# Attention and routed experts on one core: a group's output product in two passes of 256 tokens, weights' halves side by side

## The chip, the cores and the metric

The kernel runs on one core of a Trainium2 chip. The metric is the device time of one execution in microseconds (us). Three runs of the kernel before took 1854.25, 1854.31 and 1855.54 us; the median is 1854.31 us. A fourth, profiled execution took 1854.06 us, and all rows below are from it. The engines are named as the profile names them: PE is TensorE (matmuls; PEld are its weight loads), DVE is VectorE, ACT is ScalarE, POOL is GpSimd, SP is the engine that issues most DMAs.

## The reference

There are two stages. The first is attention of 4 x 12288 queries on 768 pooled keys; the second sends each token to one of 8 experts.

```
kv_flat = mean over 4x4 patches of kv @ w_sr            # k = v = kv_flat, 768 x 128 for each of 4 batches
s = (q @ k.T) / sqrt(128);  a = softmax(s);  x = a @ v  # 4 x 12288 tokens of 128
e_idx = argmax(x @ w_gate);  gate_w = softmax(x @ w_gate)[e_idx];  eom = sigmoid(x @ w_output_gate)
h  = relu(x[e] @ w1[e])                                  # 128 -> 1024
ye = h @ w2[e]                                           # 1024 -> 128
out[e] = gate_w * eom[e] * ye                            # for the tokens whose e_idx is e
```

## The kernel before

Tokens come in 96 groups of 512 (`GT`), 24 groups to a batch (`GPB`). The kernel guesses one expert for each batch, the one that most of its tokens choose, and runs all tokens of the batch through it; the few tokens with another expert are listed by indirect DMAs and done in small tiles at the end. Every fp32 product is made of fp16 parts: a number is held as a high half and a low half, and a product is high by high, high by low and low by high.

Three products of a group fill PE: the scores S (per block of 128 tokens 6 matmuls of 384 columns), the attention's output U (18 matmuls of 512 columns), and the expert. The expert has two: H, per block f of 128 of the 1024 hidden features 3 matmuls of 512 columns (`moe_h`, L938 to L940), and Y, the output product (`moe_y`, L948 to L977). For H, ACT writes the high half HH (`Relu`, L943), and DVE the low half HL (L945); both are 128x512 in fp16, in rings of 5 tiles each. For Y, HH and HL are the stationary operands: per f and per block j of 128 tokens, HH is multiplied with the high half of w2 and, in a second matmul with the same HH loaded again, with its low half; then HL with the high half of w2. These 12 matmuls of 128 columns all add into the same 128 columns of j. Four j of 128 fp32 fill one PSUM bank, tile Y of the pool psY, which has that one buffer. After the eighth f, ACT copies Y to `ys` in SBUF (L977), and Y is free for the next group. PSUM has eight banks: four for S (two tiles of two banks, psA), three for H and U (psH) and one for Y.

```
for j in range(GB):                       # L964 to L968
    for h in range(2):
        add(Y[:, ts(j, P)], HH[:, ts(j, P)], w2[:, h, :], ...)
for j in range(GB):
    add(Y[:, ts(j, P)], HL[:, ts(j, P)], w2[:, 0, :])
```

After the last attention group there is another form, called wide: the banks of S are free then, so Y takes two of them, and one matmul of 256 columns multiplies HH with both halves of w2, which lie side by side; the two results stand in different columns, and ACT (L974) and DVE (L975) add them.

Order is written out by hand. The main loop runs over groups i, with 8 slots s each; a slot issues, in the order of `cfg.ORD` = "shxryfue", the scores of a block of 128 (in even slots), one block of H, the exponential (even) or the rounding (odd), one block of Y, half of U (slots 5 and 6) and waiting events. Every engine runs its own instructions in the order in which they are issued. `hb` and `yb` count the blocks of H and Y. Y follows H by 4 blocks (5 for the first of a group); the last three blocks of a group come at the start of a slot, ahead of the scores. A group's H starts two groups after its attention (`LAG`), and one slot in 30 (one in 8 from group 72 on) has no H. When the attention is over, the last groups' H and Y are still open and follow by themselves. `moe_scale` (L985) multiplies `ys` with the gates 8 groups after the attention of its group, in the second half of a group's slots; `moe_out` stores it. `w_load` (L835) fetches an expert's weights.

Of the kernel before, what the change touches and what calls it, by code (L numbers as in the profile page):

```python
# [20 lines left out]
F32 = mybir.dt.float32  # L21
F32R = mybir.dt.float32r
F16 = mybir.dt.float16
# [98 lines left out]
def body(ctx, tc, q, kv, w_sr, w_gate, w_og, w1, w2, out, cfg=Cfg):  # L122
# [104 lines left out]


    kvst = {}
    KVN = [[0, 0] for _ in range(NB)]  # L230
# [312 lines left out]
    def qk(i, j):  # L543
# [288 lines left out]

    MSC, WT, WW2, HS, YP, OST, OT = {}, {}, {}, {}, {}, {}, {}
# [100 lines left out]
    def moe_h(i, f):  # L934
        w1h, w1l = WT[i // GPB][0:2]
        UH, UL = US[i]
        H = psH.tile([P, GT], F32, tag="H", name=f"H{i}_{f}")
        pe.matmul(H, w1h[:, ts(f, P)], UH, start=True, stop=False)  # L938
        pe.matmul(H, w1h[:, ts(f, P)], UL, start=False, stop=False)  # L939
        pe.matmul(H, w1l[:, ts(f, P)], UH, start=False, stop=True)  # L940
        HH = wk.tile([P, GT], F16, tag="HH", bufs=5, name=f"HH{i}_{f}")
        HL = wk.tile([P, GT], F16, tag="HL", bufs=5, name=f"HL{i}_{f}")
        ins = act.activation(HH, H, AF.Relu)  # L943
        pace[:] = [getattr(ins, "ins", ins).name]
        dve.scalar_tensor_tensor(HL, H, 0.0, HH, op0=ALU.max, op1=ALU.subtract)  # L945
        HS[(i, f)] = (HH, HL)

    def moe_y(i, f):  # L948
        HH, HL = HS.pop((i, f))
        if f == 0:  # L950
# [9 lines left out]
        for j in range(GB):  # L960
            if wide:
                add(Y[:, j // 2, ts(j % 2, 2 * C)], HH[:, ts(j, P)], w2, f == 0 and j % 2 == 0)
                continue
            for h in range(2):  # L964
                add(Y[:, ts(j, P)], HH[:, ts(j, P)], w2[:, h, :], f == 0 and j == 0 and h == 0)
        for j in range(GB):
            add(Y[:, j // 2, j % 2 * 2 * C:j % 2 * 2 * C + C] if wide else Y[:, ts(j, P)],
                HL[:, ts(j, P)], w2[:, 0, :])  # L968
        if f == NFB - 1:
            ys = wk.tile([P, GB, C], F32, tag="ys", bufs=OL + 2, name=f"ys{i}")  # L970
# [8 lines left out]
            del US[i]  # L979

# [159 lines left out]
    with tc.manual_schedule(engines={pool.engine, sp.engine, pe.engine, act.engine, dve.engine}):  # L1140
# [22 lines left out]
        tix, tgen = [], []  # L1163
        om = NG - OL - 1
        begun = False
# [115 lines left out]

        kl, kp, hb, yb = first()
        tpre = None

# [22 lines left out]
        for i in range(3, NG + OL + 1):  # L1307
# [5 lines left out]
            for s in range(8):  # L1313
# [6 lines left out]
                go = mi >= 0 and not (att and ((8 * i + s) % cfg.SK == cfg.SO if i < 72 else (8 * i + s) % 8 == 3))  # L1320
                for _ in range(1 + (cfg.YF and yb % 8 == 6)):
                    if go and yb % 8 >= 5 and yb < 8 * NG:
                        moe_y(*divmod(yb, 8))
                        yb += 1
                for o in cfg.ORD:
                    if o == "h" and go:
                        if hb < 8 * NG:
                            moe_h(*divmod(hb, 8))
                            hb += 1
                    if o == "s" and att and s % 2 == 0:  # L1330
                        qk(i, s // 2)
# [15 lines left out]
                    if o == "y" and go and yb == hb - 4 - (cfg.YE and hb < 8 * NG and yb % 8 == 0):  # L1347
                        for _ in range(1 + (yb == hb - 5)):
# [45 lines left out]
                routes(0, att and mi >= 0 and s % 2 == 1)  # L1394
                if not att and s % 2 and om < NG and om in OST and unit[om][0] in MSC:
                    moe_scale_all(om)
                    om += 1
                if NU - 1 in SCT and not tix:
# [49 lines left out]
```

## Time and profile before

| | us |
|---|---|
| median of three runs | 1854.31 |
| the profiled execution | 1854.06 |
| its span, first to last instruction | 1852.4 |
| PE busy in the span | 1820.7 (98%), 16465 matmuls |
| PEld busy | 1187.6 (64%) |
| DVE busy | 1451.5 (78%) |
| ACT busy | 1316.6 (71%) |
| POOL busy | 1323.3 (71%) |
| TensorE's granted clock over the span | 0.999 of full speed |

The gap between the span and the execution's time is 1.66 us. A PE row's own duration is modelled and overlaps that of the next; what a matmul takes is read from the distance between starts.

### The profile page before, as it was taken

To read this page: it belongs to the slowest core of one execution; us is meant where nothing else is said; L and a number is where in the kernel's file an instruction comes from. 1 tells how busy PE (TensorE), PEld (TensorE's weight loads), DVE (VectorE), ACT (ScalarE), POOL (GpSimd) and SP (SyncE) were. 2 spreads that over 40 slices of the span, in tenths; PEclk is the share of its full clock that TensorE was granted. 3 is DMA by queue.
4 is the path that set the end of the run, shared out by engine and by line. 5 is a ranking of instruction groups with operands and counts; after the bars stand their busy time and mean duration, and the time that the engine had idled before them with its cause. 6 is when DMAs were issued, how large, how long until landed. Compare 5 with 4: busy or idle time off the path is not lost. (4 is left out here: it accounts for less than half of the span.)

```text
span 1852.4 us, 43920 instructions
## 1 busy us (share of the span) xinstructions
PE 1820.7 (98%) x16465; PEld 1187.6 (64%) x16465; DVE 1451.5 (78%) x2856; ACT 1316.6 (71%) x2367; POOL 1323.3 (71%) x1563
## 2 busy tenths in 40 slices
PE   6999999999999999999999999999999999999998
PEld 5566666666666666666666666666666666666666
DVE  6876887788878777788787787878887777787774
ACT  4777777777776777777777776767687777777644
POOL 4546877866888878768588787786687786786841
PEclk9999999999999999999999999999999999999999
DMA  8999989989998988989988999888989899887822
GB/s 253 165 171 167 183 157 191 168 159 190 185 181 175 180 178 161 187 157 181 174 177 178 183 183 178 182 155 168 178 170 168 173 172 170 158 168 155 135 64 74
DMA packets 884070, 312.47 MB, mean 169 GB/s; under 512 B 827584, under 2 KB 833857, under 8 KB 883856
## 3 DMA queue, kind: packets, MB, share of 16 engines
q1 hardware_dynamic: 870944, 309.18, 85.4%
q0 software_dynamic: 12480, 0.40, 0.6%
q8 instruction: 130, 2.13, 0.5%
q14 instruction: 84, 0.69, 0.1%
q10 hardware_dynamic: 432, 0.07, 0.0%
HBM read 56.83 MB, written 51.25 MB: 58 GB/s over the span
## 5 line engine op out<-in xcount | busy, mean ns | idle before, releaser
L140 POOL TENSOR_TENSOR ph<-pr,ph 128x384 f16<-128x384 f32 x764 | 707.0, 926 | 335.4 <-issue 265.8
L945 DVE SCALAR_TENSOR_TENSOR HL<-H,HH 128x512 f16<-128x512 f32 x768 | 526.2, 686 | 162.4 <-ACT HH L943 151.9
L943 ACT ACTIVATE HH<-H 128x512 f16<-128x512 f32 x768 | 456.6, 595 | 265.5 <-PE H L940 255.7
L579 ACT ACTIVATE pr<-S,nm,qm 128x768 f32<-128x768 f32 x384 | 380.8, 992 | 188.0 <-DVE nm L568 170.9
L958 PEld LDWEIGHTS <-HH 128*128 128x128 f16 x5952 | 393.1, 98 | 139.8 <-issue 0.5
L820 POOL DMA_INDIRECT scr<-rw,idx x384 | 387.9, 1010 | 119.7 <-issue 62.7
L958 PE MATMUL Y<-w,HH 128*128 128x128 f16 (+1 forms) x5952 | 467.8, 221 | 0.2 <-ACT ys L977 0.2
L567 DVE TENSOR_REDUCE nm<-S 128x1 f32<-128x768 f32 x384 | 363.7, 947 | 71.5 <-PE S L565 69.8
L626 PE MATMUL U<-PT,V 128*128 128x512 f16 (+1 forms) x1746 | 404.3, 377 | 8.6 <-DMA PT<-ph 3.9
L596 ACT ACTIVATE ph<-pr 128x768 f16<-128x768 f32 x380 | 320.1, 842 | 1.2
L565 PE MATMUL S<-K,qT 128*128 128x384 f16 x1536 | 312.3, 326 | 0.0
L958 PE MATMUL Y<-w,HL 128*128 128x128 f16 x3072 | 296.9, 219 | 0.0
L938 PE MATMUL H<-U,w 128*128 128x512 f16 x768 | 291.0, 379 | 1.7 <-DVE HL L945 1.6
L939 PE MATMUL H<-U,w 128*128 128x512 f16 x768 | 291.0, 379 | 0.5 <-DVE U L631 0.5
L940 PE MATMUL H<-U,w 128*128 128x512 f16 x768 | 291.1, 379 | 0.2 <-POOL w L140 0.2
L626 PEld LDWEIGHTS <-V 128*128 128x128 f16 x1746 | 166.1, 98 | 189.8 <-issue 10.6
L565 PEld LDWEIGHTS <-qT 128*128 128x128 f16 x1536 | 150.1, 98 | 99.8 <-issue 0.4
L958 PEld LDWEIGHTS <-HL 128*128 128x128 f16 x3072 | 205.8, 98 | 1.2
L562 PE MATMUL S<-K,qT 128*128 128x384 f16 x768 | 187.6, 326 | 4.7 <-ACT pr L579 4.5
L631 DVE SCALAR_TENSOR_TENSOR U<-U,U 128x512 f16<-128x512 f32 x96 | 66.4, 692 | 91.4 <-ACT U L630 91.3
L940 PEld LDWEIGHTS <-w 128*128 128x128 f16 x768 | 75.1, 98 | 91.9 <-issue 0.8
L140 POOL TENSOR_TENSOR kvs<-kvs 128x256 f32<-128x256 f32 (+2 forms) x150 | 112.8, 752 | 24.1 <-DMA kvs<-in_kv_dram 13.1
(207 smaller groups left out, 1451.5 us busy)
## 6 DMA issues: line engine op xcount, KB each, us to landing
kvs<-in_kv_dram SPq DMA_DIRECT2D x96, 256.0 KB
q<-in_q_dram SPq DMA_DIRECT2D x96, 256.0 KB
urows<-uT SPq DMA_DIRECT2D x96, 256.0 KB
out_dram<-ys SPq DMA_DIRECT2D x96, 256.0 KB
PT<-ph SPq DMA_TRANSPOSE x384
scr<-rw,idx POOLq DMA_INDIRECT x384
wr<-in_moe_w_dram SPq DMA_DIRECT2D x8, 512.0 KB
tw<-in_moe_w_dram SPq DMA_DIRECT2D x4, 512.0 KB
```

The costliest lines, as they stand in the source:

```text
L140: ins = pool.tensor_tensor(*a, **k)
L565: pe.matmul(S[:, h, 0:384], x, k[:, ts(h, 384)], start=False, stop=(n == 1))
L567: dve.tensor_reduce(out=nm[:, 0:1], in_=S[:, :, 0:384], op=ALU.max, axis=AX.XY, negate=True)
L579: act.activation(pr.rearrange("p (a k) -> p a k", a=2), S[:, :, 0:384], AF.Exp, bias=nm[:, 1:2], scale=es, accum_out=SUMS[c][:, bl:bl + 1])
L596: act.activation(ph[:, 0, :], PR[(i, j)], AF.Copy)
L626: pe.matmul(PVP[i][:, cols], ops[n][0], ops[n][1][:, cols], start=(n == 0), stop=(n == len(ops) - 1))
L820: ins = pool.indirect_dma_start(out=scr, out_offset=bass.IndirectOffsetOnAxis(ap=idx[:, bl:bl + 1], axis=0), in_=rw[:, bl, :], in_offset=None,
L938: pe.matmul(H, w1h[:, ts(f, P)], UH, start=True, stop=False)
L940: pe.matmul(H, w1l[:, ts(f, P)], UH, start=False, stop=True)
L943: ins = act.activation(HH, H, AF.Relu)
L945: dve.scalar_tensor_tensor(HL, H, 0.0, HH, op0=ALU.max, op1=ALU.subtract)
L958: pe.matmul(o, h, w, start=first, stop=(f == NFB - 1), skip_group_check=True)
```

## The change

While the attention runs, a group's Y is made in two passes of 256 tokens (`moe_y2`). In a pass the one bank holds two blocks j, with 256 columns each: the first 128 for w2's high half and the next 128 for its low half, as in the wide form. HH is loaded once and multiplied with both halves in one matmul of 256 columns; HL with w2's high half adds into the first 128. After the eighth f of a pass, ACT copies the low part of the bank to `ys`, and DVE adds the high part to it; then the bank is free for the second pass. Group 0 and the groups that begin after the attention keep the old forms; in the built program 87 groups have the new one. Since a pass needs one half of the tokens of all eight f, HH and HL are no longer 5 tiles of 512 each: they are half tiles in one buffer HB, rings of 10 for the first 256 tokens and of 16 for the others. The order of Y follows a table `TY` of half blocks: two f go together as one step u, four steps make a pass, and after each pass come two slots with no Y. Beside that, `moe_scale` goes by a counter `sc` that waits for `ys` to be there, and an expert's weights are fetched into a buffer of `stg` (that of the kv staging) and not into one of their own.

```
@@ qk: which group is scaled
-        m = i - OL - 1
-        scale = (lambda: moe_scale(m, 2 * j - 4, 2 * j - 2)) if j >= 2 and m >= 0 else None
+        m = sc[0]
+        scale = None
+        if j >= 2 and (m in OST and m <= i - OL - 1 and j == 2 or j == 3 and sc[1]):
+            scale = lambda: moe_scale(m, 2 * j - 4, 2 * j - 2)
+            sc[1] = j == 2
+            sc[0] += j == 3
@@ rings
+    N1, N2, YSB = 10, 16, OL + 2
+    HB = cst.tile([P, 2, N1 + N2, GT // 2], F16, name="HB")
@@ w_load
-        t = kvp.tile([P, 2, FF], F32, tag="wr", bufs=1, name=f"wr{b}")
+        t = kvp.tile([P, 2, FF], F32, tag="stg", name=f"wr{b}")
@@ moe_h
-        HH = wk.tile([P, GT], F16, tag="HH", bufs=5, name=f"HH{i}_{f}")
-        HL = wk.tile([P, GT], F16, tag="HL", bufs=5, name=f"HL{i}_{f}")
+        a, b = (8 * i + f) % N1, N1 + (8 * i + f) % N2
+        HH, HL = (HB[:, h, a:b + 1:b - a, :] for h in range(2))
+        H = H.rearrange("p (h x) -> p h x", h=2)
...
+    def halved(i):
+        return HV.setdefault(i, 0 < i and now[0] < 8 * NG)
+
+    def moe_y2(i, u):
+        h, n = divmod(u, 4)
+        if u % 4 == 0:
+            YP[i] = (psY.tile([P, GT], F32, tag="Y", name=f"Y{i}_{h}") if now[0] < 8 * NG else
+                     psA.tile([P, 2, 512], F32, tag="A", name=f"Y{i}_{h}")[:, 0, :]).rearrange("p (j h c) -> p j h c", j=2, h=2)
+        Y = YP[i]
+        for f in (2 * n, 2 * n + 1):
+            HH, HL = (x[:, h, :] for x in HS[(i, f)])
+            w2 = WW2[i // GPB][:, :, ts(f, P)]
+            for j in range(2):
+                pe.matmul(Y[:, j, :, :], HH[:, ts(j, P)], w2, start=(f == 0 and j == 0), stop=(f == NFB - 1), skip_group_check=True)
+            for j in range(2):
+                pe.matmul(Y[:, j, 0, :], HL[:, ts(j, P)], w2[:, 0, :], start=False, stop=(f == NFB - 1), skip_group_check=True)
+        if n == 3:
+            if h == 0:
+                OS2[i] = wk.tile([P, GB, C], F32, tag="ys", bufs=YSB, name=f"ys{i}")
+            ys = OS2[i][:, 2 * h:2 * h + 2, :]
+            act.activation(ys, Y[:, :, 1, :], AF.Copy)
+            dve.tensor_tensor(ys, Y[:, :, 0, :], ys, op=ALU.add)
+            del YP[i]
+            if h:
+                OST[i] = OS2.pop(i)
+
     def moe_y(i, f):
+        if halved(i):
+            return moe_y2(i, f)
...
@@ main loop, start of a slot (hc counts the blocks of H as hb does)
+        TY = [16, 17, 19, 20, 24, 25, 27, 28]
-                for _ in range(1 + (cfg.YF and yb % 8 == 6)):
-                    if go and yb % 8 >= 5 and yb < 8 * NG:
+                if go and halved(yb // 8):
+                    while now[0] < 8 * NG and halved(yb // 8) and 16 * (yb // 8) + TY[yb % 8] <= 2 * hc:
                         moe_y(*divmod(yb, 8))
                         yb += 1
...
@@ main loop, the place "y" behind H
+                    if o == "y" and go and halved(yb // 8):
+                        if now[0] < 8 * NG:
+                            while halved(yb // 8) and 16 * (yb // 8) + TY[yb % 8] <= 2 * hc - 1:
+                                moe_y(*divmod(yb, 8))
+                                yb += 1
...
-                if s == cfg.MO and oi - 1 in OT:
-                    moe_out(oi - 1)
+                if s == cfg.MO and OT:
+                    moe_out(next(iter(OT)))
```

How the change moves instructions is seen at three places. The first is PE in group 31, the first block of its Y. Before, each pair of rows is one load of a slice of HH and one matmul of 128 columns, and a slice is loaded twice (once for each half of w2):

```order
L958 LDWEIGHTS HH31_0_10267
L958 MATMUL Y31_10405<-w11_7058,HH31_0_10267 128x128
L958 LDWEIGHTS HH31_0_10267
L958 MATMUL Y31_10405<-w11_7058,HH31_0_10267 128x128
L958 LDWEIGHTS HH31_0_10267
L958 MATMUL Y31_10405<-w11_7058,HH31_0_10267 128x128
L958 LDWEIGHTS HH31_0_10267
L958 MATMUL Y31_10405<-w11_7058,HH31_0_10267 128x128
```

Now a block f of one pass is whole in eight rows: two matmuls of 256 columns with HH and two of 128 with HL, both read from HB (Y31_0 is the first pass of group 31).

```order
L979 LDWEIGHTS HB_138
L979 MATMUL Y31_0_9140<-w11_6130,HB_138 128x256
L979 LDWEIGHTS HB_138
L979 MATMUL Y31_0_9140<-w11_6130,HB_138 128x256
L981 LDWEIGHTS HB_138
L981 MATMUL Y31_0_9140<-w11_6130,HB_138 128x128
L981 LDWEIGHTS HB_138
L981 MATMUL Y31_0_9140<-w11_6130,HB_138 128x128
```

A block of all 512 tokens had 12 loads and 12 matmuls, and has 8 of each. The second place is ACT's queue where Y of group 31 is copied out; H32 is the H of the next group, pr the exponential of the scores and ph its rounded form. Before:

```order
L943 ACTIVATE HH32_0_10580<-H32_0_10576 128x512
L579 ACTIVATE pr35_0_10584,SUM32_9620<-S35_0_10565,nm35_0_10573,qm8_8141 128x768
L358 ACTIVATE kT2_7484,vs2_7486<-S35_0_10565 128x128
L772 ACTIVATE z7_10462<-z7_10462 128x16
L943 ACTIVATE HH32_1_10612<-H32_1_10608 128x512
L596 ACTIVATE ph35_0_10616<-pr35_0_10584 128x768
L977 ACTIVATE ys31_10635<-Y31_10405 128x512
L943 ACTIVATE HH32_2_10653<-H32_2_10649 128x512
```

Now the first pass of group 31 is copied at the same place, with half the size; the second pass has a copy of its own 12 rows on.

```order
L960 ACTIVATE HB_138<-H32_0_9161 128x2x256
L584 ACTIVATE pr35_0_9167,SUM32_8337<-S35_0_9150,nm35_0_9158,qm8_7073 128x768
L359 ACTIVATE kT2_6504,vs2_6506<-S35_0_9150 128x128
L777 ACTIVATE z7_9068<-z7_9068 128x16
L960 ACTIVATE HB_138<-H32_1_9187 128x2x256
L601 ACTIVATE ph35_0_9193<-pr35_0_9167 128x768
L986 ACTIVATE ys31_9216<-Y31_0_9140 128x256
L960 ACTIVATE HB_138<-H32_2_9231 128x2x256
```

ACT's queue is otherwise the same. The third place is DVE's queue at the same point; nm is the largest score of a row, z the routing's. Now:

```order
L962 SCALAR_TENSOR_TENSOR HB_138<-H32_1_9187,HB_138 128x2x256
L779 SCALAR_TENSOR_TENSOR z7_9068<-z7_9068,sume7_8727 128x16
L780 SCALAR_TENSOR_TENSOR z7_9068<-se7_8985,z7_9068 128x16
L987 TENSOR_TENSOR ys31_9216<-Y31_0_9140,ys31_9216 128x256
L572 TENSOR_REDUCE nm35_1_9228<-S35_1_9219 128x1
L573 TENSOR_SCALAR nm35_1_9228<-nm35_1_9228,qm8_7073 128x1
L962 SCALAR_TENSOR_TENSOR HB_138<-H32_2_9231,HB_138 128x2x256
```

The row of L987 is new, twice in a group: DVE adds the two parts of a pass, ahead of the next scores' largest and of the next HL. PE's first matmul of the following pass waits for it.

## Rows read from the trace of the kernel before

**Rows 1.** The page: span, and busy us, share and count of PE.

```profile
span 1852.4 us, 43920 instructions
...
PE 1820.7 (98%) x16465; PEld 1187.6 (64%) x16465; DVE 1451.5 (78%) x2856; ACT 1316.6 (71%) x2367; POOL 1323.3 (71%) x1563
```

**Rows 2.** Busy us by stretch; then granted clock, DMA share, GB/s.

```profile
1400.00:1600.00 200.00, 200.00 (x1809) 128.31 (x1807) 157.80 (x303) 149.56 (x261) 147.42 (x173) 1.00 0.91 170
```

**Rows 3.** PE in order of time: start, us, tiles, count; two blocks of Y.

```profile
902.50 0.61 PE L958 MATMUL Y<-w,HH 128*128 128x128 f16 x8
...
903.84 0.49 PE L562 MATMUL S<-K,qT 128*128 128x384 f16 x2
...
904.81 0.38 PE L938 MATMUL H<-U,w 128*128 128x512 f16 x1
...
905.46 0.61 PE L958 MATMUL Y<-w,HH 128*128 128x128 f16 x8
...
906.78 2.11 PE L626 MATMUL U<-PT,V 128*128 128x512 f16 x9
908.72 0.50 PE L958 MATMUL Y<-w,HH 128*128 128x128 f16 x6
```

**Rows 4.** PE in order of time near the end: two blocks of the wide form.

```profile
1820.85 0.60 PE L958 MATMUL Y<-w,HH 128*128 128x256 f16 x4
...
1822.17 0.38 PE L938 MATMUL H<-U,w 128*128 128x512 f16 x1
```

**Rows 5.** Groups by line and shape: count, busy us, mean ns, idle before.

```profile
L958 PE MATMUL Y<-w,HH 128*128 128x128 f16 x5760 | 439.1, 219 | 0.2 <-ACT ys L977 0.2
...
L567 DVE TENSOR_REDUCE nm<-S 128x1 f32<-128x768 f32 x384 | 363.7, 947 | 71.5 <-PE S L565 69.8
...
L985 DVE TENSOR_TENSOR ys<-ys,msw 128x256 f32<-128x256 f32 x176 | 105.0, 596 | 0.0
...
L985 DVE TENSOR_TENSOR ys<-ys,msw 128x512 f32<-128x512 f32 x8 | 5.5, 684 | 1.0 <-ACT ys L977 1.0
...
L975 DVE TENSOR_TENSOR ys<-Y,ys 128x512 f32<-128x512 f32 x6 | 4.2, 692 | 0.0
```

**Rows 6.** The copy of Y (line 977): durations in ns, first and last.

```profile
L977 ACT ACTIVATE ys<-Y x90: 576/593/605, 72.2 to 1839.0; 128x512 f32<-128x512 f32 x90
```

**Rows 7.** Waits: who waited for whom, us in total, times, longest.

```profile
ACT ys L977 <- PE Y L958: 6.0, 6, 2.3
...
PE U L626 <- DVE q L512: 2.0, 1, 2.0
...
PE H L938 <- DVE HL L945: 1.6, 4, 0.6
...
PE U L626 <- DVE HL L945: 1.4, 3, 0.7
```

**Rows 8.** All engines in order of time: an ordinary copy of Y.

```profile
679.45 0.61 PE L958 MATMUL Y<-w,HH 128*128 128x128 f16 x8
...
680.12 0.38 PE L938 MATMUL H<-U,w 128*128 128x512 f16 x1
...
680.30 0.99 ACT L579 ACTIVATE pr<-S,nm,qm 128x768 f32<-128x768 f32 x1
...
681.29 0.59 ACT L977 ACTIVATE ys<-Y 128x512 f32<-128x512 f32 x1
```

**Rows 9.** The same about a late copy, among the routing's operations.

```profile
1251.76 1.58 DVE L774 SCALAR_TENSOR_TENSOR z<-z,sume 128x16 f32<-128x16 f32 x1
...
1252.13 0.61 PE L958 MATMUL Y<-w,HH 128*128 128x128 f16 x8
...
1252.80 0.38 PE L938 MATMUL H<-U,w 128*128 128x512 f16 x1
...
1255.68 0.59 ACT L977 ACTIVATE ys<-Y 128x512 f32<-128x512 f32 x1
...
1256.32 0.38 PE L958 MATMUL Y<-w,HH 128*128 128x128 f16 x4 [0.20 <-ACT ys L977]
```

More of the change, by code (lines that the diff above doesn't have):

```diff
@@ L226, in body @@
     qscale = float(C) ** -0.5
+    sc, HV = [0, False], {}
     kvst = {}
@@ L830, in routing, with ready @@
             yield
-    MSC, WT, WW2, HS, YP, OST, OT = {}, {}, {}, {}, {}, {}, {}
+    MSC, WT, WW2, HS, YP, OST, OT, OS2 = {}, {}, {}, {}, {}, {}, {}, {}
+    N1, N2, YSB = 10, 16, OL + 2
+    HB = cst.tile([P, 2, N1 + N2, GT // 2], F16, name="HB")
+    def ready(yb, hb):
+        i, u = divmod(yb, 8)
+        if not halved(i):
+            return hb - yb
+        return hb - yb if hb < 8 * NG else hb - 8 * i - 2 * (u % 4) - 2 + LG_
+    LG_ = 8
     def w_load(b, ei):
         r = sp.value_load(ei[0:1, 0:1], min_val=0, max_val=E - 1)
-        t = kvp.tile([P, 2, FF], F32, tag="wr", bufs=1, name=f"wr{b}")
+        t = kvp.tile([P, 2, FF], F32, tag="stg", name=f"wr{b}")
         sp.dma_start(out=t[:, 0, :], in_=w1[bass.ds(r, 1), :, :].rearrange("o d f -> d (o f)"))
@@ L961, in moe_y @@
             if wide:
-                add(Y[:, j // 2, ts(j % 2, 2 * C)], HH[:, ts(j, P)], w2, f == 0 and j % 2 == 0)
+                add(Y[:, j // 2, ts(j % 2, 2 * C)], HH[:, j // 2, ts(j % 2, P)], w2, f == 0 and j % 2 == 0)
                 continue
             for h in range(2):
-                add(Y[:, ts(j, P)], HH[:, ts(j, P)], w2[:, h, :], f == 0 and j == 0 and h == 0)
+                add(Y[:, ts(j, P)], HH[:, j // 2, ts(j % 2, P)], w2[:, h, :], f == 0 and j == 0 and h == 0)
         for j in range(GB):
             add(Y[:, j // 2, j % 2 * 2 * C:j % 2 * 2 * C + C] if wide else Y[:, ts(j, P)],
-                HL[:, ts(j, P)], w2[:, 0, :])
+                HL[:, j // 2, ts(j % 2, P)], w2[:, 0, :])
         if f == NFB - 1:
-            ys = wk.tile([P, GB, C], F32, tag="ys", bufs=OL + 2, name=f"ys{i}")
+            ys = wk.tile([P, GB, C], F32, tag="ys", bufs=YSB, name=f"ys{i}")
             del YP[i]
@@ L978, in moe_y @@
             OST[i] = ys
-            del US[i]
     def moe_scale(i, a, b):
@@ L1163, in body @@
         tix, tgen = [], []
-        om = NG - OL - 1
         begun = False
@@ L1282, in body @@
         kl, kp, hb, yb = first()
+        hc = hb
+        TY = [16, 17, 19, 20, 24, 25, 27, 28]
         tpre = None
@@ L1320, in body @@
                 go = mi >= 0 and not (att and ((8 * i + s) % cfg.SK == cfg.SO if i < 72 else (8 * i + s) % 8 == 3))
-                for _ in range(1 + (cfg.YF and yb % 8 == 6)):
-                    if go and yb % 8 >= 5 and yb < 8 * NG:
+                if go and halved(yb // 8):
+                    while now[0] < 8 * NG and halved(yb // 8) and 16 * (yb // 8) + TY[yb % 8] <= 2 * hc:
                         moe_y(*divmod(yb, 8))
                         yb += 1
+                elif go and yb % 8 >= 5 and yb < 8 * NG:
+                    moe_y(*divmod(yb, 8))
+                    yb += 1
                 for o in cfg.ORD:
@@ L1329, in body @@
                             hb += 1
+                            hc += 1
                     if o == "s" and att and s % 2 == 0:
@@ L1346, in body @@
                                 pv(pvi, lo, hi)
-                    if o == "y" and go and yb == hb - 4 - (cfg.YE and hb < 8 * NG and yb % 8 == 0):
-                        for _ in range(1 + (yb == hb - 5)):
+                    if o == "y" and go and halved(yb // 8):
+                        if now[0] < 8 * NG:
+                            while halved(yb // 8) and 16 * (yb // 8) + TY[yb % 8] <= 2 * hc - 1:
+                                moe_y(*divmod(yb, 8))
+                                yb += 1
+                        else:
+                            for _ in range(2):
+                                if halved(yb // 8) and hb >= 8 * (yb // 8) + 2 * (yb % 4) + 4:
+                                    moe_y(*divmod(yb, 8))
+                                    yb += 1
+                    elif o == "y" and go and yb <= hb - 4 - (cfg.YE and hb < 8 * NG and yb % 8 == 0):
+                        for _ in range(1 + (yb <= hb - 5)):
                             moe_y(*divmod(yb, 8))
@@ L1394, in body @@
                 routes(0, att and mi >= 0 and s % 2 == 1)
-                if not att and s % 2 and om < NG and om in OST and unit[om][0] in MSC:
-                    moe_scale_all(om)
-                    om += 1
+                if not att and s % 2 and sc[0] in OST and unit[sc[0]][0] in MSC:
+                    moe_scale_all(sc[0])
+                    sc[0] += 1
                 if NU - 1 in SCT and not tix:
```

## The prediction

> **What bounds the kernel now.** I read the page first, for the engine that has no rest: PE, with 98% of the span busy against 78% for the next engine [rows 1]. A PE row's duration is modelled, so the busy share alone proves little; the second view is therefore busy time by stretch, where PE is busy for 200.00 of 200 us at full granted clock [rows 2]. The third is PE in order of time, where the reader is to measure from start to start and not to read the durations. Two blocks of Y, 24 matmuls of 128 columns, take 903.84 - 902.50 = 1.34 us, so 55.8 ns each; nine matmuls of U, 512 columns, take 908.72 - 906.78 = 1.94 us, 215.6 ns each [rows 3]. No gap is left between them, and the same holds for S (0.97 us for a block of scores) and H (0.65 us, from 904.81 to 905.46). So in the main loop the time is the sum of the matmuls' distances, and an edit counts by what it takes from that sum and by the waits that it puts into it. The fourth view, the waits, says how often PE is held up by a late engine: H and U waited for DVE for 1.6 + 1.4 + 2.0 = 5.0 us in all [rows 7], and Y waited for its copy for 0.2 us in all [rows 5].
>
> **The change, part by part.**
>
> *Fewer matmuls.* A line through the two distances gives (215.6 - 55.8) / 384 = 0.416 ns for a column, and 55.8 - 128 x 0.416 = 2.5 ns that every matmul costs whatever its width. A matmul of 256 columns then takes 109.1 ns where two of 128 take 111.6. The wide form near the end shows it directly: two of its blocks, with the same columns but 16 matmuls for 24, take 1822.17 - 1820.85 = 1.32 us [rows 4], which is 0.02 us less for 8 matmuls, again 2.5 ns each. 87 groups lose 32 matmuls each, 2784 in all: 2784 x 2.5 ns = 7.0 us, all of it on the path. Rounding of the rows (0.01 us at each end) leaves 5 to 9 us.
>
> The Trainium skill speaks of another size here. "TensorE: Matmul & The Clock Gate", section Back-to-back issue gap, says that in a stream of pairs of weight load and matmul both set the spacing, and gives about 81 ns for 128 columns. Here 24 such pairs run at 55.8 ns, so the loads lie wholly beside the matmuls, and the measurement decides; by the Trainium skill's figure a matmul taken away would be worth 25 ns more, and the sum some 70 us lower.
>
> *The copy of Y.* Before, one copy of 512 columns on ACT, 593 ns [rows 6]. Now two of 256 in a group; each lies between half of that, 0.30, and all of it, 0.59 us. I take 0.37, near the lower end, since only the fixed part doesn't halve. ACT has 29% of the span idle [rows 1], so the 0.15 us more per group cost nothing by themselves.
>
> *The sum of the two parts on DVE.* New, twice in a group. The nearest rows are the same addition in the wide form, 692 ns for 512 columns, and the gates' product of 256 columns, 596 ns [rows 5]. The largest of 768 scores takes 947 ns, so a column costs about (947 - 692) / 256 = 1.0 ns, and 256 columns 0.43 us. The bounds are 0.35 (half of 692) and 0.60 us.
>
> Why is the gates' product so slow? Its form with 512 columns, which runs when POOL is nearly done, takes 684 ns [rows 5], hardly more. The Trainium skill, "SBUF — State Buffer", section Who interferes with whom, says that a DVE instruction with two inputs in SBUF contends with POOL over a shared port, and one with at most one doesn't. The new addition has one input in PSUM; by that rule it takes 0.43 us, and by the row of the gates 0.60.
>
> I take 0.43: 174 x 0.43 = 75 us (0.60 would make it 104), which brings DVE from 1451.5 to some 1527 us, 83%. That is still below PE, so the load costs nothing as load. What it can cost is delay, since DVE runs in order: behind the addition, which waits for ACT's copy, stand the largest scores and the next HL, and for these wait the exponential on ACT and, three tiles later, PE's H.
>
> *The handover of the bank.* This is the price. Before, Y was handed over once a group, after ACT's copy alone, and between the last matmul of a group and the first of the next PE had at least three blocks of H and one S, 2.92 us by the distances above. Now it is handed over twice, after ACT and DVE, and the two slots without Y hold, when no U falls in them, one S and two H: 0.97 + 2 x 0.65 = 2.27 us. About half of the 174 handovers have only this; the others have one or both halves of U (1.94 us each) or a slot without H.
>
> What the chain takes is read from copies before. ACT had to wait for Y in only 6 of 90 copies [rows 7]: in all others it was behind. An ordinary one [rows 8]: H ends at 679.45, Y at 680.12, and the copy starts at 681.29, because the exponential stands ahead of it. In the new order two steps of Y follow that H, so the pass ends at 679.45 + 1.32 = 680.77; the copy would still start at 681.29 and end at 681.66, and with 0.06 for the signal the sum would end at 682.15. PE wants the bank at 680.77 + 2.27 = 683.04: 0.9 us to spare, no wait. A late one [rows 9]: an operation of the routing holds DVE for 1.58 us, the scores' largest and so the exponential come late, and the copy starts only at 1255.68, 2.88 us after Y's end. PE waited 0.20 us. In the new order the pass ends at 1252.13 + 1.32 = 1253.45, PE wants the bank at 1255.72, and the sum ends at 1255.68 + 0.37 + 0.06 + 0.43 = 1256.54: a wait of 0.8 us.
>
> So a tight handover costs 0 or about 0.8 us. The routing comes once in four groups, 24 times. Its pile lasts about two slots of the 32 in four groups, and four tight handovers with two slots each stand in these 32, so one in four piles meets one: 6 x 0.8 = 4.8 us. The bounds are 0 (every one like rows 8) and 24 x 0.8 = 19 us (every pile meets one). I take 4.8, nearer to the ordinary row, since a copy as late as that of rows 9 is rare.
>
> *The three tiles of H and U.* The order leaves PE more work between the end of a tile and the reuse of its bank: by the distances above the least goes from 1.62 to 2.28 us for an H behind a U, and from 2.42 to 3.08 for an H behind an H. The 5.0 us of waits for DVE [rows 7] can so shrink, by 0 to 5; or DVE's new work takes as much again. I take 2.0 of gain.
>
> *At nothing:* the half tiles (the same 512 columns in two pieces; should the piece cost 20 ns, ACT's and DVE's idle time covers it); the weights in a staging buffer, whose last reader is done before the next keys want it (else SP would wait there, and behind it the transposes of P for U); the counter of `moe_scale`, which only lets a group be scaled later.
>
> *Sum,* against the profiled execution of 1854.06 us: -7.0 for the matmuls, +4.8 for the handovers, -2.0 for H and U gives 1849.9. The median of the runs is 0.25 us above that execution, so 1850.1 us.
>
> **The rivals.**
>
> *A, the handover eats more than the gain (slower).* Place: PE's first matmul of a pass, which waits for DVE's sum. If every routing pile meets a tight handover, or the ordinary margin of 0.9 us is used up wherever rounding, query turning and routing fall together, waits come to 19 us: 1854.06 - 7.0 - 2.0 + 19 + 0.25 = 1864.3. It decides from 9.0 us of waits, about 11 late handovers, where the gain is gone; from 12.7 the kernel is measurably slower. For it: ACT is behind in 84 of 90 copies. Against it: with 2.92 us of room PE waited only 0.2 us in all.
>
> *B, gain and waits cancel (no change).* 9 us of waits, 0.1 us on each tight handover: 1854.3. For and against as in A; it needs only that half of the piles collide.
>
> *C, no handover waits.* 1845.3. For it speaks rows 8; against it rows 9, which would wait.
>
> *D, the loads were the limit.* A load lasts 1187.6 us / 16465 = 72 ns in the mean [rows 1]. If each one taken away freed the 16 ns by which that exceeds the 55.8 ns of its matmul, beside the 7.0 us, the time would be 1854.06 - 7.0 - 2784 x 0.016 + 0.25 = 1802.8. Rows 3 speak plainly against it, as do rows 4, where fewer loads gain nothing beyond the 2.5 ns. The Trainium skill's figure, in the section named above, would have it so.
>
> **How the numbers follow.** Forecast 0.40, A 0.27, B 0.25, C 0.07, D 0.01. What a measurement can tell from no change is about 0.2%, 3.7 us, so faster is below 1850.6. Of the forecast, which spans 1847 to 1852 with 2 to 7 us of waits, 0.34 lies there; with C and D faster has 0.42. The rest of the forecast and most of B make 0.29 for the same; A and B's upper edge make 0.29 for slower. The range for 8 in 10 is 1845.5 to 1865; the forecast's own is 1847 to 1852.
>
> **What would show it.** PE's matmuls of Y in 256 columns at 109 ns from start to start and 2784 such rows (some may be missing) would confirm the first step; PE's rows of Y waiting for the DVE addition, 5 us in all and mostly among the routing's operations, the second; less than 5 us for H and U behind DVE the third; an addition of 0.43 us, and not 0.60, the price on DVE. I am wrong if the first matmul of a pass waits for more than 9 us in all, if DVE's late HL holds H, or if the distance of 256 columns isn't below that of two times 128.

## The result and the profile after

The changed kernel takes 1869.92 us (median of 4 runs, 1869.46 to 1870.1) where the kernel before takes 1854.28 (1853.21 to 1855.54): a ratio of 1.0084, 95% interval [1.0072, 1.0096]. It is slower by 15.6 us. The forecast was 1850.1, faster, with a range up to 1865.

The page of the changed kernel, against [rows 1]:

```profile
span 1868.4 us, 38509 instructions
...
PE 1821.3 (97%) x13649; PEld 1149.3 (62%) x13649; DVE 1502.5 (80%) x3030; ACT 1319.8 (71%) x2454; POOL 1321.3 (71%) x1563
```

There are 2816 matmuls fewer: 2784 by the two passes, and 32 because one group more falls to the wide form at the end (7 groups in place of 6). But PE's busy time hasn't gone down: a PE row's duration is modelled and swallows short waits. So again PE in order of time, start to start (start, us, tiles, count), as in [rows 3]:

```profile
908.28 0.38 PE L979 MATMUL Y<-w,HB 128*128 128x256 f16 x2
908.50 0.27 PE L981 MATMUL Y<-w,HB 128*128 128x128 f16 x2
908.61 0.38 PE L979 MATMUL Y<-w,HB 128*128 128x256 f16 x2
908.83 0.27 PE L981 MATMUL Y<-w,HB 128*128 128x128 f16 x2
908.94 0.38 PE L979 MATMUL Y<-w,HB 128*128 128x256 f16 x2
909.15 0.27 PE L981 MATMUL Y<-w,HB 128*128 128x128 f16 x2
909.27 0.38 PE L979 MATMUL Y<-w,HB 128*128 128x256 f16 x2
909.49 0.27 PE L981 MATMUL Y<-w,HB 128*128 128x128 f16 x2
909.60 0.49 PE L567 MATMUL S<-K,qT 128*128 128x384 f16 x2
```

Sixteen matmuls take 909.60 - 908.28 = 1.32 us, as in the wide form [rows 4], where 24 of the old form took 1.34 [rows 3]; two of 256 columns take 0.22. The gain of 2.5 ns for each matmul is there. Where nothing is late, PE still has no rest (first row, against [rows 2], same columns); in the second stretch it rests for 4.2 of 200 us, against 0.5 before:

```profile
1400.00:1600.00 200.00, 200.00 (x1493) 124.65 (x1492) 165.40 (x328) 149.51 (x274) 149.66 (x174) 1.00 0.92 169
400.00:600.00 200.00, 195.85 (x1470) 122.44 (x1469) 164.66 (x332) 144.11 (x268) 150.99 (x176) 1.00 0.89 173
```

The groups of the new form (count, busy us, mean ns, idle time before and what ended it), against [rows 5]:

```profile
L572 DVE TENSOR_REDUCE nm<-S 128x1 f32<-128x768 f32 x384 | 363.5, 947 | 37.8 <-PE S L570 35.3
...
L1030 DVE TENSOR_TENSOR ys<-ys,msw 128x256 f32<-128x256 f32 x174 | 101.3, 582 | 0.0
L987 DVE TENSOR_TENSOR ys<-Y,ys 128x256 f32<-128x256 f32 x174 | 72.7, 418 | 54.3 <-ACT ys L986 51.7 <-ACT kT L359 0.4
...
L986 ACT ACTIVATE ys<-Y 128x256 f32<-128x256 f32 x174 | 65.9, 379 | 8.1 <-PE Y L981 7.1
```

The addition lasts 418 ns (0.43 was forecast), the copy 379 (0.37). What the prediction has no number for is the last column of L987: before the addition DVE stands idle for 51.7 us, until ACT's copy. In return it now stands 35.3 us for the scores where it stood 69.8 [rows 5]: DVE arrives later. PE's waits (us in total, times, longest), against [rows 7]:

```profile
PE Y L979 <- DVE ys L987: 10.3, 17, 1.1
...
PE U L631 <- DVE HB L962: 4.6, 7, 1.1
...
PE U L631 <- DVE q L513: 3.9, 1, 3.9
PE H L954 <- DVE HB L962: 2.7, 6, 1.0
```

These understate it, since the modelled end hides some 0.16 us of every wait. I therefore took, over all of PE, each start-to-start distance, subtracted the median distance of the same kind of row, and summed what exceeds it by more than 25 ns, by the tile that came late. Before: 24.4 us (U 10.6, S 5.5, H 4.2, Y 0.5, others 3.6). After: 45.5 us (Y 14.7, U 14.4, S 6.5, H 6.3, others 3.6). So -7.0 us of matmuls and +21.1 of waits give +14.1, of the 1868.4 - 1852.4 = 16.0 us that the spans differ by.

These sums leave out one stretch, in which matmuls took longer and nobody was late. In the changed kernel no matmul starts on PE between 74.25 and 78.55 us, and then it runs at the lower of its two clock levels (granted clock 0.50, 1.2 GHz) until 84.3 us. PE in order of time, and a row by stretch (columns as in [rows 2]), first after, then before:

```profile
74.25 0.38 PE L956 MATMUL H<-U,w 128*128 128x512 f16 x1
78.55 4.00 PE L631 MATMUL U<-PT,V 128*128 128x512 f16 x9 [3.92 <-DVE q L513]
82.34 0.85 PE L567 MATMUL S<-K,qT 128*128 128x384 f16 x2
82.98 1.46 PE L570 MATMUL S<-K,qT 128*128 128x384 f16 x4
84.26 0.40 PE L954 MATMUL H<-U,w 128*128 128x512 f16 x1
79.00:82.00 3.00, 3.00 (x9) 1.07 (x8) 0.13 (x1) 0.14 (x1) 2.55 (x3) 0.50 1.08 206
...
78.91 2.10 PE L626 MATMUL U<-PT,V 128*128 128x512 f16 x9 [2.02 <-DVE q L512]
80.85 0.49 PE L562 MATMUL S<-K,qT 128*128 128x384 f16 x2
79.00:80.80 1.80, 1.80 (x9) 0.79 (x9) 0.69 (x1) 1.01 (x2) 0.66 (x1) 1.00 0.67 119
```

Nine matmuls of U take 3.79 us there and 1.94 before, and a block of scores 1.92 and 0.97: 2.8 us lost. With them the sum is +16.9, which is 0.9 more than the spans differ by. This place belongs to the new order of Y, which leaves PE no block of Y ahead of that U, and not to the addition: e9_cadence below, which has the order alone, waits 3.9 us there too and then has a granted clock of 0.50.

One of the late handovers in full, in order of time (an idle time and its releaser in brackets):

```profile
427.33 1.52 DVE L729 TENSOR_TENSOR oh<-t,m 128x128 f32<-128x128 f32 x1
...
428.09 0.28 PE L981 MATMUL Y<-w,HB 128*128 128x128 f16 x2
...
428.71 0.93 DVE L572 TENSOR_REDUCE nm<-S 128x1 f32<-128x768 f32 x1
...
429.92 0.99 ACT L584 ACTIVATE pr<-S,nm,qm 128x768 f32<-128x768 f32 x1 [2.24 <-DVE nm L573]
...
430.90 0.37 ACT L986 ACTIVATE ys<-Y 128x256 f32<-128x256 f32 x1
...
431.31 0.42 DVE L987 TENSOR_TENSOR ys<-Y,ys 128x256 f32<-128x256 f32 x1 [0.44 <-ACT ys L986]
...
431.79 0.38 PE L979 MATMUL Y<-w,HB 128*128 128x256 f16 x2 [1.15 <-DVE ys L987]
431.80 0.69 DVE L962 SCALAR_TENSOR_TENSOR HB<-H,HB 128x512 f16<-128x512 f32 x1
```

It is the pattern of [rows 9]: an operation of the routing holds DVE for 1.52 us, the scores' largest come late, the exponential waits 2.24 us for them, the copy behind it starts 2.8 us after Y's last matmuls. Now DVE stands 0.44 us for that copy and PE waits 1.15 us. The next HL stands behind the addition in DVE's order; here it starts when ACT's HH is there. Of the 23 waits of Y over 0.1 us between 100 and 1750 us, 17 have an operation of the routing (lines 721 to 786) among DVE's last six before the addition; they fall on 14 stretches of the routing's 24.

### The profile page after: what moved, and what is told of

Read it like the earlier page. It is cut to its first block, busy times and chain, and to the rows that moved or that the text cites. A ratio compares the mean times of both kernels' runs of the same rounds, so it can differ in the third digit from the quotient of the medians.

```text
span 1868.4 us, 38509 instructions
## 1 busy us (share of the span) xinstructions
PE 1821.3 (97%) x13649; PEld 1149.3 (62%) x13649; DVE 1502.5 (80%) x3030; ACT 1319.8 (71%) x2454; POOL 1321.3 (71%) x1563
## 5 line engine op out<-in xcount | busy, mean ns | idle before, releaser
L962 DVE SCALAR_TENSOR_TENSOR HB<-H,HB 128x512 f16<-128x512 f32 x768 | 525.5, 685 | 120.3 <-ACT HB L960 110.2
L960 ACT ACTIVATE HB<-H 128x512 f16<-128x512 f32 x768 | 455.9, 594 | 225.0 <-PE H L956 219.7
L979 PE MATMUL Y<-w,HB 128*128 128x256 f16 x2784 | 488.9, 273 | 10.7 <-DVE ys L987 10.3
L572 DVE TENSOR_REDUCE nm<-S 128x1 f32<-128x768 f32 x384 | 363.5, 947 | 37.8 <-PE S L570 35.3
L981 PE MATMUL Y<-w,HB 128*128 128x128 f16 x2784 | 382.5, 219 | 0.2 <-DVE HB L962 0.2
L979 PEld LDWEIGHTS <-HB 128*128 128x128 f16 x2784 | 237.4, 98 | 147.6 <-issue 17.0
L981 PEld LDWEIGHTS <-HB 128*128 128x128 f16 x2784 | 272.2, 98 | 32.0 <-DVE HB L962 0.5
L631 PEld LDWEIGHTS <-V 128*128 128x128 f16 x1746 | 166.6, 98 | 195.5 <-issue 18.2
```

What stands on the lines that cost most here:

```text
L572: dve.tensor_reduce(out=nm[:, 0:1], in_=S[:, :, 0:384], op=ALU.max, axis=AX.XY, negate=True)
L631: pe.matmul(PVP[i][:, cols], ops[n][0], ops[n][1][:, cols], start=(n == 0), stop=(n == len(ops) - 1))
L979: pe.matmul(Y[:, j, :, :], HH[:, ts(j, P)], w2, start=(f == 0 and j == 0), stop=(f == NFB - 1), skip_group_check=True)
L981: pe.matmul(Y[:, j, 0, :], HL[:, ts(j, P)], w2[:, 0, :], start=False, stop=(f == NFB - 1), skip_group_check=True)
```

## The experiments

The ratio is always to the kernel before in the same sitting. The level of that kernel moved between sittings, 1854.6 and 1854.9 us in two and 1863.95 to 1865.25 in the others, so ratios within 0.2% are compared only at one level (A the lower, B the upper). At B the changed kernel stands at 1.0063 [1.0046, 1.008]. "Waits" are the start-to-start sums between 100 and 1750 us; the kernel before has 8.8 there, the changed kernel 27.1 (both traced at A; at B the changed kernel has 31.8, and the kernel before was not traced).

In the expectations theory 1 is the bank's handover, 2 DVE's load, 3 the rings and what came with them, 4 DVE's standing for ACT's copy, 5 the new order of Y. From e15_both on the handover has the number 5, and 6 is load and standing together. U is the product of the attention weights with the values and takes a bank of the same three as H; where an expectation calls late tiles "the router's" or "the gate's", H and U are meant.

**e1_rings**: the rings, the weights' buffer and the counter, with every group in the old form.

```
 def halved(i):
-    return HV.setdefault(i, 0 < i and now[0] < 8 * NG)
+    return False
```

> Everything of the change but the two passes: half-tile rings, the counter of the gates' scaling, the weights in a staging buffer; every group keeps the old form of Y with 12 matmuls of 128 columns a block. Theory 1 (the bank's handover costs the time) and theory 2 (DVE's additional load costs it) both expect the time of the kernel before, 1854 us within 2 us, since neither the handover nor the load is there. Theory 3 (the rings, the staging buffer or the later scaling cost it) expects more than 1860 us.

1.0003 [0.9993, 1.0012] at A. They cost nothing; theory 3 falls.

**e9_cadence**: the new order of Y, every group in the old form (`moe_y` no longer calls `moe_y2`).

> The cadence alone: the steps of Y in the order of the changed kernel's table (16, 17, 19, 20, 24, 25, 27, 28), but each step is one block of the old form, 512 tokens in 12 matmuls of 128 columns, one copy a group by ACT and no addition. PE's work at each place is the same but for the 2.5 ns a matmul. Theory 4 expects the time before, 1853 to 1857. Theory 5 expects most of the loss, 1864 to 1878.

1.0008 [0.9998, 1.0018] at B. The order alone is not the loss, though its trace has the wait and the low clock near 78 us; the kernel before was not traced at B, so what sets them off is open.

**e7_noadd**: the changed kernel without the addition (the product with the low half of w2 is left out).

```
-act.activation(ys, Y[:, :, 1, :], AF.Copy)
-dve.tensor_tensor(ys, Y[:, :, 0, :], ys, op=ALU.add)
+act.activation(ys, Y[:, :, 0, :], AF.Copy)
```

> The changed kernel without DVE's addition: ACT copies the high part of a pass and the low part is left out of the result. The two passes, their order and ACT's copies stay. Theory 4 (DVE stands still in its own queue until ACT's copy is there, 52 us in the changed kernel's trace, beside 73 us of additions, and so HL and U's split come late) expects a kernel faster than before, by the 7 us of the matmuls: 1847 to 1851. Theory 5 (the uneven cadence of PE, four steps of Y in little more than a slot and then two blocks of H without Y, makes ACT and DVE late) expects 1864 to 1872.

0.9967 [0.9955, 0.998] at B, waits 14.5 us, 4.6 of them for Y, which here waits for ACT's copy alone. The gain that the matmuls promised is real, and the addition alone turns it into a loss of 0.96% between this kernel and the changed one. Everything after this is about which property of the addition does it.

**e2_load**: before, with two DVE reductions of 256 columns of a constant in a group.

```
+if f in (3, NFB - 1) and i > 0:
+    dve.tensor_reduce(out=dm, in_=dz..., op=ALU.max, axis=AX.X)
```

> The kernel before with two DVE reductions of 256 columns more in each group but the first, at the fourth and the last block of Y; they read a constant in SBUF, nobody waits for their result and they wait for nothing. This is DVE's additional load (about 0.4 us each, 78 us in all) without a handover. Theory 1 (the handover) expects at most 3 us over the kernel before, 1854 to 1857. Theory 2 (DVE's load delays the low halves of H and U, and PE waits for these) expects most of the loss seen, 1864 to 1872, with PE's rows of H and U waiting.

1.0019 [1.001, 1.0029] at A: 77.3 us of load, more than the addition's, and DVE at 81%. As load alone it costs 3.3 us, between the bands of the two theories.

**e3_nohand**: copy and addition read a constant, so PE never waits for them (Y is left out of the result).

```
-act.activation(ys, Y[:, :, 1, :], AF.Copy)
-dve.tensor_tensor(ys, Y[:, :, 0, :], ys, op=ALU.add)
+act.activation(ys, dz, AF.Copy)
+dve.tensor_tensor(ys, dz, ys, op=ALU.add)
```

> The changed kernel, but ACT's copy and DVE's addition of a pass read a constant in SBUF and not the bank, so PE never waits for them at the start of a pass (the output product's result is left out for 87 groups). ACT's and DVE's loads stay, the addition being rather longer with both inputs in SBUF. Theory 1 expects the handover's waits gone, 14.7 us by the trace of the changed kernel (24 waits of 0.6 us), so 1853 to 1857. Theory 2 expects the time to stay at 1866 to 1873.

1.0093 [1.0076, 1.011] at A, no better. PE's waits:

```profile
PE U L631 <- DVE HB L964: 14.6, 16, 5.0
...
PE H L956 <- DVE HB L964: 6.2, 16, 0.9
```

Y's waits are gone (0.5 us), and U's and H's have taken their place (25.1 us by start to start). But the addition lasted 632 ns with both inputs outside PSUM, 37 us more in all, so this run alone doesn't acquit the handover.

**e4_ty18**: three slots between the passes for two.

```
-TY = [16, 17, 19, 20, 24, 25, 27, 28]
+TY = [18, 18, 20, 20, 26, 26, 28, 28]
```

> The changed kernel with another table for the steps of Y, 18, 18, 20, 20, 26, 26, 28, 28: two steps ahead of the same H and two ahead of the next, so a pass is over within one slot and three slots without Y lie between two passes, not two. The least room for a handover rises from 2.27 to 2.92 us, what it was before the change. Theory 1 expects most of the 14.7 us of waits for Y gone, 1856 to 1860. Theory 2 expects 1867 to 1872, as no load is taken away.

1.0111 [1.0094, 1.0127] at A: Y 0.6 us, U 20.3, H 11.5. The room that Y was given is missing between H and U.

**e6_reduce**: DVE reduces the bank alone, without ACT's copy.

```
-act.activation(ys, Y[:, :, 1, :], AF.Copy)
-dve.tensor_tensor(ys, Y[:, :, 0, :], ys, op=ALU.add)
+dve.tensor_reduce(out=ys, in_=Y.rearrange("p j h c -> p j c h"), op=ALU.add, axis=AX.X)
```

> The changed kernel with DVE alone at the end of a pass: one reduction over the two parts, 512 columns read from the bank, about 0.69 us, and no copy by ACT. DVE's load is 47 us larger than in the changed kernel, but it waits for PE alone and not for ACT's queue. Theory 4 expects 1854 to 1862, clearly faster than the changed kernel. Theory 2 (load) expects it slower, 1872 to 1885. Theory 5 expects about the changed kernel's 1870.

1.0051 [1.0034, 1.0068] at B; 679 ns each, 118.1 us of DVE, which hardly stands before it (6.1 us). Y still waits 18.2 us for the bank. Standing was exchanged for load, at about the same price.

**e8_defer**: ACT copies the whole bank, DVE adds a slot later outside PSUM (571 ns).

```
-act.activation(ys, Y[:, :, 1, :], AF.Copy)
-dve.tensor_tensor(ys, Y[:, :, 0, :], ys, op=ALU.add)
+act.activation(yt, Y, AF.Copy)
+at(1, total)   # total: dve.tensor_tensor(ys, yt[:, :, 0, :], yt[:, :, 1, :], op=ALU.add)
```

> The changed kernel with the addition made later: ACT copies the whole bank (512 columns) to SBUF, which frees it, and DVE adds the two parts in SBUF one slot later, when the copy is long done. DVE's load is at least as large (0.6 us an addition with both inputs in SBUF), ACT's is larger by 0.2 us a pass, but DVE never stands still for the copy. Theory 4 expects 1849 to 1857. Theory 2 (load alone) expects no gain, 1868 to 1876. Theory 5 (cadence) expects 1866 to 1872.

1.0096 [1.0079, 1.0112] at B. No standing, no handover through DVE, but Y waits 16.0 us for the longer copy (592 ns) and U 14.6.

**e12_pool**: the same with the addition on POOL (`pool_tt`).

> ScalarE copies the whole bank into a buffer (512 columns, as in the kernel with the deferred addition, 1.0096), and GpSimd adds the two halves one slot later, in VectorE's place. Theories 2 and 4 alike: VectorE is freed, so the loss goes, and what is left is ScalarE's longer copy (some 28 us of busy time on an engine that is busy for 71% of the span) and 174 additions on GpSimd, also busy for 71%: 0.998 to 1.003. If GpSimd's own lateness is passed on (its pieces of the router's and the values' work), or if the bank is handed over later, 1.005 to 1.012.

1.0169 [1.0152, 1.0186] at B, a miss for every theory: 766 ns each, 133.4 us on POOL, Y waits 22.5 us for the copy, U 13.4, H 12.6. POOL was not free either.

**e10_load7, e11_stand**: e7_noadd with, in the addition's place, the load without standing, or the standing without load.

```
+dve.tensor_reduce(out=dm, in_=dz..., op=ALU.max, axis=AX.X)   # e10
+dve.tensor_copy(dm, ys[:, 0, 0:1])                              # e11
```

> Leaves out the addition of the bank's second half (the low part of the weights is missing in the result) and puts in its place a VectorE reduction of 256 columns of a constant, 0.41 us, 174 of them: the same load at the same place of VectorE's order, but it waits for nobody and nobody waits for it. The kernel without the addition stood at 0.9967 of the kernel before, the changed kernel at 1.0084. Theory 2 (the load of 73 us itself, in an order in which VectorE is late anyway, makes the loss): back at 1.005 to 1.009, and the high part of H (SUBTRACT after Relu) and the gate's product are late for the score product and the router's, U and H together over 15 us of waits. Theory 4 (VectorE stands 52 us for ScalarE's copy and that standing makes the loss): 0.997 to 0.999.

> As the kernel without the addition, with a VectorE copy of one column of the tile that ScalarE has just copied in its place: VectorE stands for ScalarE's copy as in the changed kernel, but does next to nothing afterwards (some 0.1 us, 174 of them: 15 us in all). Theory 4 (the standing makes the loss): 1.004 to 1.008, some 45 us of VectorE's idle time in front of that copy, and TensorE's waits for U and H at 15 us or more. Theory 2 (the load makes it): 0.996 to 0.999, with the same idle time in front of the copy. Both in part: between, and the sum of this kernel's and the load alone's distances should come near 0.0117.

e10: 0.9982 [0.9973, 0.9992], e11: 1.0000 [0.999, 1.0009], both at B. The idle time before the tiny copy shows that e11 stands as the changed kernel does:

```profile
L988 DVE COPY dm<-ys 128x1 f32<-128x1 f32 x174 | 25.8, 148 | 57.9 <-ACT ys L987 51.0 <-ACT q L511 1.3 <-ACT pr L584 1.2
```

Against 0.9967 that is 0.15% for the load, which is not clear of noise (the intervals of e7 and e10 overlap), and 0.33% for the standing: neither theory 2 nor 4 by itself. Together they would leave 1.0015.

**e13_after**: the changed kernel once more.

> The changed kernel once more, beside these three on one chip: 1.0075 to 1.0095 of the kernel before by every theory, with TensorE's waits for Y, U and H at about 27 us between 100 and 1750 us, against 9 to 14 of the kernel before.

1.0063 [1.0046, 1.008] at B, somewhat less than expected; waits 31.8 us.

**e15_both, e16_hand**: e7_noadd with standing and load, or with standing and handover, in the addition's place.

```
+dve.tensor_reduce(out=dm, in_=ys..., op=ALU.max, axis=AX.X)             # e15
+dve.tensor_tensor(dm, Y[:, 0, 0, 0:1], ys[:, 0, 0:1], op=ALU.add)       # e16
```

> Leaves out the addition (the low part of the weights is missing in the result) and reduces in its place the 256 columns that ScalarE has just copied: VectorE stands for the copy and then works 0.41 us, as in the changed kernel, but the bank is free once ScalarE's copy ends. Without both: 0.9967; load alone 0.9982; standing alone 1.0000; everything 1.0063. Theory 5 (the bank's handover through VectorE makes the rest): about 1.0015, the sum of the two, with TensorE's waits for Y near 5 us as there. Theory 6 (load and standing together make VectorE late beyond their sum): 1.004 to 1.008, with waits for U and H of 18 us or more.

> Leaves out the addition (the low part of the weights is missing in the result); in its place VectorE adds one column of the bank to one column of ScalarE's copy, some 0.1 us: standing and the handover of the bank through VectorE, without the load. Theory 5 (handover): clearly over the standing alone (1.0000), 1.003 to 1.006, with waits for Y of 10 us or more. Theory 6 (load and standing together): 0.999 to 1.002.

e15: 1.0034 [1.0021, 1.0046]; Y 5.0 us, U 10.7, H 8.3. e16: 1.0018 [1.0008, 1.0027]; Y 10.7, U 7.9, H 4.3. Both theories fall short of the whole:

| addition's properties present (level B) | ratio | over e7 |
|---|---|---|
| none (e7_noadd) | 0.9967 | 0 |
| load (e10_load7) | 0.9982 | 0.15% |
| standing (e11_stand) | 1.0000 | 0.33% |
| standing, load (e15_both) | 1.0034 | 0.67% |
| standing, handover (e16_hand) | 1.0018 | 0.51% |
| all three (e13_after) | 1.0063 | 0.96% |

Each ratio is good to 0.1 to 0.17% and each difference to about 0.2%, so the parts are rough: standing some 0.33%, load 0.15% by itself and 0.34 where DVE stands as well, the handover 0.2 to 0.3%. Y's own waits bear out the handover: 4.6 to 5.2 us in the four kernels in which only ACT's copy frees the bank, 10.7 in e16 and 17.0 in e13.

**e14_slot**: the addition behind the next HL in DVE's order.

```
-dve.tensor_tensor(ys, Y[:, :, 0, :], ys, op=ALU.add)
+at(0, total)   # the same addition, at the slot's end
```

> The changed kernel with the addition put behind the next high part of H in VectorE's order, at the end of the slot in place of its beginning; ScalarE's copy stays where it was, and the bank is written again two slots after the pass. The load stays (73 us), the standing should go (52 us of VectorE's idle time in front of the addition to under 15), and the bank comes free about half a slot (2 to 3 us) later. Theory 6 and theory 4 (the standing in the queue): 0.997 to 1.000, the load alone's 0.9982 being the aim. Theory 5 (the handover): the later release makes it worse, 1.006 to 1.015, waits for Y over 17 us.

1.0725 [1.0707, 1.0743] at B, far worse than any theory had it:

```profile
PE Y L979 <- DVE ys L989: 117.7, 103, 2.7
```

DVE no longer stands before the addition, and PE waits 138.1 us for the bank in 133 places. So the handover has a hard edge. In the changed kernel the addition ends 2.1 us (median) after the last matmul of its pass begins, here 3.8 us, and the least room is 2.3: 1.7 us more, and it is late in 133 of 174 handovers. The early place of the addition in DVE's order, with its standing, is the price of being in time.

**e17_room, e18_room2**: e14_slot with three slots between the passes, by the table of e4_ty18 and by 17, 18, 19, 20, 26, 26, 27, 28.

> The whole addition, behind the next high part of H in VectorE's order, with passes that begin at 18 and 26 half slots in place of 16 and 24 (18, 18, 20, 20, 26, 26, 28, 28): three H products between one pass and the next in place of two. With the same table and the addition at its old place the kernel stood at 1.0111. If load, standing and handover are the whole loss: standing and the waits for Y go, the load stays: 0.997 to 1.001, VectorE's idle time in front of the addition under 15 us, waits for Y under 8 us. If the bunched passes (four blocks in little over a slot) make VectorE late by themselves, or the load is dearer than its 0.15% once the low part is computed: 1.004 to 1.012, with waits for U and H of 15 us or more.

> As the kernel with three slots between the passes, by a table that bunches the first pass less (17, 18, 19, 20, 26, 26, 27, 28). Load, standing and handover as the whole loss: 0.997 to 1.001, within 0.002 of the other table. Bunching as a cause of its own: better than the other table by 0.003 or more.

1.0103 [1.0086, 1.012] and 1.0138 [1.0121, 1.0155] at A. e18, which bunches less, is the slower one, against both of its expectations (Y 19.8 us, U 13.9). There is no standing and, in e17, little waiting for Y (7.3 us); but U waits 19.7:

```profile
PE U L631 <- DVE HB L962: 18.4, 19, 4.7
...
PE Y L979 <- DVE ys L989: 4.5, 8, 1.2
```

**e19_bunch**: e7_noadd with the table of e4_ty18.

> Leaves out the addition (the low part of the weights is missing in the result), with passes that begin at 18 and 26 half slots as in the kernel with three slots of room. Without the addition and with the table of the changed kernel: 0.9967. If the wider table costs by itself: 1.003 to 1.007, with waits of TensorE for U of 12 us or more between 100 and 1750 us. If the addition's load is needed for that: 0.996 to 0.999, U at 5 to 8 us.

1.0001 [0.9992, 1.0011] at B: under the band expected of the table as a cause of its own, over the other; U 16.3 us against 5.6, Y 0.4. The wider table loses some 0.3% without any addition; that blocks of Y moved next to one another no longer stand between an H and the reuse of its bank would explain U's waits, but was not tried by itself. It is about a quarter of e17's distance from e7, roughly, since the two were run at different levels; the rest comes with the addition behind HL, and how it divides was not tried. No version that computes everything beat the kernel before.

## Why the prediction was wrong

- *Fewer matmuls, -7.0 us*: right. 1.32 us for two blocks, and 0.9967 once the addition is gone. By an estimate from the Trainium skill's figure ("TensorE: Matmul & The Clock Gate", Back-to-back issue gap) the sum would have been some 70 us lower; no run shows that. Rival D is out: by it the two blocks would have taken 1.34 - 8 x 0.0185 = 1.19 us.
- *The copy and the addition*: 379 and 418 ns, as taken. The addition does not depend on what POOL does beside it: it takes 418 ns (median) in the 69 cases with no arithmetic of POOL beside it and 424 in the others, while the gates' product of 256 columns, with both inputs in SBUF, takes 415 ns in the 46 cases without and 860 where POOL is at work for over 90% of it. The Trainium skill's rule ("SBUF — State Buffer", Who interferes with whom), that a DVE instruction with at most one input in SBUF is spared the contention with POOL, agrees with these rows.
- *"The load costs nothing as load"*: this step failed. Load alone costs 0.19% [0.10, 0.29] in the old order, and in the new one 0.15%, not clear of noise, or 0.34% where DVE stands as well, though DVE is idle for a fifth of the span. And the sentence on delay, which named the HL and the scores behind the addition, put no price on it: DVE stands 51.7 us for ACT's copy, 0.33%, and with the load on top 0.67%.
- *The handover, 4.8 us*: the mechanism was right, the size wrong. Y's waits are 14.7 us, a mean of 0.6 in 24 places where 6 of 0.8 were taken. I worked out how late the old kernel's DVE would be and how often a tight pass falls into that; the changed DVE is later, and 14 of the 24 stretches of routing have a late handover. That is most of the way to rival A (every pile, 19 us).
- *H and U, -2.0 us*: wrong in sign. They rose by 3.8 + 2.1 = 5.9 us. Of this 1.9 is U's wait near 78 us, where the new order leaves PE nothing to do. In the rest the larger distance on PE, which should have relieved them, was more than used up by DVE's later HL (waits of U and H for it 4.6 + 2.7 us, before 1.4 + 1.6).
- *At nothing*: rings, buffer and counter, 0.03%: right. TensorE's clock had no term at all; the stretch at granted clock 0.50 behind the wait near 78 us cost 2.8 us.

So the slower rival had the right side and mechanism (1864.3), but it kept the relief of 2.0 us. With 14.2 more for Y, +5.9 for H and U, +1.0 for S and 2.8 for the clock, the sum is 1854.1 - 7.0 + 14.2 + 6.9 + 2.8 + 0.25 = 1871.2, 1.3 over the 1869.92 measured; that is what the method leaves open. Not settled is what part of DVE's lateness starts at which operation: the routing's small operations last up to 1.9 us in these rows, and no run took them apart.

## What to carry to other kernels

An engine that works in order and sits between two others is not priced by its share of busy time. Add up what a new instruction stands for, then what it works, and ask who is served after it; here 52 us of standing and 73 of work on an engine at 80% cost more than 2784 matmuls gave back. And where PE has no rest, room between two uses of a bank is taken from another bank's room: test the handover, the standing and the load each by itself before moving the order.

## What the runs showed of the hardware

- The kernel before ran at 1854 to 1855 us in some sittings and at 1864 to 1865 in others. Its traces are all from the lower level, but those of the changed kernel (1868.4 us at A, 1874.4 in e13_after) differ in the built program: the text is the same, yet waits stand at other instructions. In 14 places of e13_after DVE's largest scores wait, by the profile, for the next H, 1.4 us in the mean; such waits (4 to 20) are in every trace at B and in none at A. That they are the whole of the difference is not shown.

```profile
DVE nm L572 <- PE H L956: 19.0, 14, 2.1
```

- After 4.3 us with no matmul started, PE ran at granted clock 0.50: a matmul of 512 columns took 427 ns from start to start and one of 384 took 320, against 216 and 162 at 1.00. In the kernel before, after the shorter wait (2.0 us) at the same place, the clock stayed at 1.00.
- On DVE, adding 256 columns of f32 cost 418 ns with one input in PSUM, and 571 to 632 in the mean with both in SBUF while POOL was 70% busy; a reduction of 256 columns with one input cost 406 to 413; one column alone costs 148 to 153 ns. The same addition on POOL took 766 ns.
